# The low part of the last 64 activation rows, as 64-row products for two output blocks at once

## The chip, the cores and the metric

The kernel runs on one core of a Trainium2 chip. The metric is the device time of one execution in microseconds (us), and the median of several runs is quoted. Engines are named as in the profile: PE is TensorE (PEld its weight loads), DVE is VectorE, ACT is ScalarE, POOL is GpSimd and SP is SyncE, which issues most DMA transfers.

## The reference, cut to what matters

A recurrent attention gives 3072 rows of 320 features. Two expert layers follow; the change is in the second.

```python
def _moe_ref(x, w1, w2, w3, w_out):                 # d_ff 768
    h = np.maximum(np.maximum(x @ w1, x @ w2), x @ w3)
    return (h @ w_out).astype(np.float32)

def _moe2_ref(x, w_a, w_b, w_out):                  # d_ff 1536
    a = x @ w_a
    b = x @ w_b
    return (a * b @ w_out).astype(np.float32)
```

## The kernel before, in words

**Two parts of every number.** The weights arrive in 64-bit floats and the activations in 32-bit. Products are made in the 32-bit type fp32r, which TensorE takes at one column a step but rounds. So each operand is split into a high part and a low part, and a product is the sum of high x high, low x high and high x low.

**The second expert** (`moe_b(n)`, line 1039) runs for six groups n of 512 rows of x. The 320 features are the contraction: 128 + 128 + 64. The first two blocks have tiles `bxhi` and `bxlo` for the activations' parts and `bw` for the weights'. The last 64 features stand twice, in partitions 0 to 63 and again in 64 to 127: `bxt` holds their high part and `bxl` their low part. The matching weight tile `bt` holds the high part of the weights in partitions 0 to 63 and the low part in 64 to 127, so that one product over 128 partitions adds high and low weights at once.

For each of 12 blocks ff of 128 hidden units the work is:

- `l3` twice (line 1061), once for w_a and once for w_b: eight products of 512 columns that sum into one PSUM bank, six with `bw`, then `bt` with `bxt`, then `bt` with `bxl`;
- ACT copies the first bank (line 1087), DVE multiplies it with the second (line 1088), ACT makes the high part `bgh` (line 1090) and DVE the low part `bgl` by a subtraction (line 1091);
- `l4` (line 1072): twelve products of 320 columns into four output banks that stay open over all 12 blocks.

PSUM has eight banks: four for the outputs, four for the first products.

**Weights.** Of the 12 blocks, nine are split during the attention, written to DRAM and loaded again by `weights_b` (line 1018). The last three are split on the spot by `live_b` (line 1028) through `pieces` (line 846): four conversions of the raw 64-bit words on DVE (lines 841 to 844), copies of the high parts on ACT (lines 861 and 863), subtractions and additions for the low parts (lines 878 and 879). With two raw tiles a block this is sixteen DVE instructions.

**The order.** All work is entered as operations with costs, keys that are read and written, and priorities; `Plan.run` then lays them out greedily and emits each engine's instructions in that order. An operation that needs PSUM banks (`ps`) is placed only when it can have all of them, and banks of kind "b" are limited to four. When the planner expects PE to stand idle before its 650th microsecond, it emits fill: 128x128 products of the identity with itself into a free bank (line 320). They are ordinary instructions that PE has to run. A tile change is charged through the mark `md`.

Of the kernel before, what the change touches and what calls it, by code (L numbers as in the profile page):

```python
# [8 lines left out]
F32 = mybir.dt.float32  # L9
# [17 lines left out]
LV = 9  # L27
# [41 lines left out]
class Plan:  # L69
# [30 lines left out]
    def run(self, limit):  # L100
# [27 lines left out]
        done, last, top = 0, 0, 0.0  # L128
        line, port, mode = 0.0, 0.0, None
        itime, ileft = 0.0, ICAP  # L130
        count = lambda o: 0 if not o["md"] else 64 if o["md"] == "c64" and o["act"] > 0.42 else 128
        busy = {}

        state = [False]
# [147 lines left out]
def body(nc, tc, ia, out_ap):  # L282
# [17 lines left out]
    def dma(fn, nbytes, r=(), w=(), pri=0.0, pre=1.2):  # L300
        return op("SP", XISS, fn, r=r, w=w, pri=pri, lat=XWAY, pre=pre, xfer=nbytes / XRATE)
# [544 lines left out]
    def pieces(src, m, raw, ca, kr, ka, parts, WK, pri, summed=False, behind=None, need=()):  # L846

        rv = lambda: raw().bitcast(U32)[:, 0:2 * m].rearrange("p (m k) -> p m k", k=2)
        f = lambda k, c, n, r0, q: rv()[r0:r0 + q, c:c + n, k].bitcast(F32)
        if behind is None:  # L850
            dma(lambda w_: SP.dma_start(rv(), src.bitcast(U32).rearrange("p (m k) -> p m k", k=2)), 128 * m * 8, r=list(need), w=[kr], pri=pri)
        else:
            adma(lambda w_: A.dma_start(rv(), src.bitcast(U32).rearrange("p (m k) -> p m k", k=2)), 128 * m * 8, w=[kr], pri=pri, after=[behind])
        convert(rv, ca, m, kr, ka, pri)
        for i, (h, l, c, n, r0, q) in enumerate(parts):
            W = WK[i] if isinstance(WK, list) else WK
            k = (kr, "h", i)
            g_ = (lambda v: v.rearrange("p (k c) -> p k c", k=2)) if n > 512 else (lambda v: v)
            f = lambda k, c, n, r0, q, g_=g_: g_(rv()[r0:r0 + q, c:c + n, k].bitcast(F32))
            a = lambda c=c, n=n, r0=r0, q=q, g_=g_: g_(ca()[r0:r0 + q, c:c + n])  # L860
            last = op("ACT", ac(n), lambda w_, f=f, h=h, c=c, n=n, r0=r0, q=q: A.activation(h(), f(1, c, n, r0, q), AF.Copy), r=[kr], w=[k, W], pri=pri)
            if r0:
                op("ACT", ac(n), lambda w_, f=f, l=l, c=c, n=n, r0=r0, q=q: A.activation(l(), f(1, c, n, r0, q), AF.Copy), r=[kr], w=[k, W], pri=pri)
                h = l
            if summed:

                pn = ("a", "cv", next(serial))
                ro = 64 if q == 64 else 0
                o_ = lambda w_, pn=pn, n=n, ro=ro, q=q: bank[w_[pn]][ro:ro + q, 0:n]
                op("PE", n * 0.0035, lambda w_, f=f, h=h, c=c, n=n, r0=r0, q=q, o_=o_: (  # L870
                    T.matmul(o_(w_), ident[r0:r0 + q, r0:r0 + q], f(1, c, n, r0, q), start=True, stop=False),
                    T.matmul(o_(w_), nid[r0:r0 + q, r0:r0 + q], h().bitcast(F32), start=False, stop=False)),
                   r=[kr, k, "nid", "con"], w=[pn], ps=[pn], pri=pri, act=0.9)
                op("PE", n * 0.00175, lambda w_, f=f, c=c, n=n, r0=r0, q=q, o_=o_: T.matmul(o_(w_), ident[r0:r0 + q, r0:r0 + q], f(0, c, n, r0, q), start=False, stop=True),
                   r=[kr, "con"], w=[pn], pri=pri, act=0.9)
                op("ACT", ac(n), lambda w_, l=l, o_=o_: A.activation(l(), o_(w_), AF.Copy), r=[pn], w=[W, k], fin=[pn], pri=pri)
                continue
            sub = lambda E, f=f, h=h, a=a, c=c, n=n, r0=r0, q=q: (lambda w_: E.tensor_tensor(a(), f(1, c, n, r0, q), h(), ALU.subtract))
            add = lambda E, f=f, l=l, a=a, c=c, n=n, r0=r0, q=q: (lambda w_: E.tensor_tensor(l(), a(), f(0, c, n, r0, q), ALU.add))
            op("POOL", po(n), sub(G), r=[kr, k], w=[ka], pri=pri, alt=[("DVE", dv(n), sub(V))])  # L880
            op("POOL", po(n), add(G), r=[kr, ka], w=[W], pri=pri, alt=[("DVE", dv(n), add(V))])
        return last
# [81 lines left out]
    def bweights(w, k, nw):  # L964
        tb["bw", k] = w.tile([128, nw, 2, 512], F32R, name=f"bw{k}")
        tb["bt", k] = w.tile([128, nw, 256], F32R, name=f"bt{k}")
        tb["bo", k] = w.tile([128, nw, 2, DM], F32R, name=f"bo{k}")

    def wb(t, ff):
# [48 lines left out]
    def weights_b():  # L1018
        need = ["WB"]
        for ff in range(LV):  # L1020
            d = [("WD", ff, 0, i) for i in range(2)]
            dma(lambda w_, ff=ff: SP.dma_start(wb("bw", ff).bitcast(F32), WD[ff, :, :, 0:512].rearrange("k p c -> p k c")), 524e3, r=d + need, w=[("bW", ff)], pri=0.7)
            for i in range(2):
                dma(lambda w_, ff=ff, i=i: SP.dma_start(wb("bt", ff).bitcast(F32)[64 * i:64 * i + 64].rearrange("p (w c) -> p w c", w=2),
                                                        WD[ff, i, :, 512:640].rearrange("(w p) c -> p w c", w=2)), 66e3, r=d + need, w=[("bT", ff, i)], pri=0.7)
            dma(lambda w_, ff=ff: SP.dma_start(wb("bo", ff).bitcast(F32), WD[ff, :, :, 640:960].rearrange("k p c -> p k c")), 328e3, r=d + need, w=[("bO", ff)], pri=0.7)

    def live_b():

        for ff in range(LV, 12):  # L1030
            for q, (c0, m) in enumerate(((0, 512), (512, 448))):
                if q == 0:
                    parts = [(lambda ff=ff: wb("bw", ff)[:, 0], lambda ff=ff: wb("bw", ff)[:, 1], 0, 512, 0, 128)]
                else:
                    parts = [(lambda ff=ff, w=w: wb("bt", ff)[0:64, 128 * w:128 * w + 128], lambda ff=ff, w=w: wb("bt", ff)[64:128, 128 * w:128 * w + 128], 0, 128, 64 * w, 64) for w in range(2)]
                    parts.append((lambda ff=ff: wb("bo", ff)[:, 0], lambda ff=ff: wb("bo", ff)[:, 1], 128, DM, 0, 128))
                pieces(ia["wpb"][ff][:, c0:c0 + m], m, lambda q=q: tb["lr", q], lambda q=q: tb["lc", q], ("lr", q), ("lc", q), parts, ("bL", ff, q), 0.5, need=["WB"] if ff < NW else ["XB"])

    def moe_b(n):
# [21 lines left out]
        def l3(w_, ff, wi, pn):  # L1061
            ps = bank[w_[pn]]
            bh, bl = (wb("bw", ff)[:, k].rearrange("p (k c) -> p k c", k=2) for k in range(2))
            t2 = wb("bt", ff)
            cs = slice(wi * 128, wi * 128 + 128)
            h, l = tb["xhi", i], tb["xlo", i]
            seq = [(bh[:, 0, cs], h[:, 0]), (bh[:, 1, cs], h[:, 1]), (bl[:, 0, cs], h[:, 0]), (bl[:, 1, cs], h[:, 1]),
                   (bh[:, 0, cs], l[:, 0]), (bh[:, 1, cs], l[:, 1]), (t2[:, cs], tb["xt2", i]), (t2[:, cs], tb["xl2", i])]
            for k, (w, x) in enumerate(seq):
                T.matmul(ps, w, x, start=(k == 0), stop=(k == 7))  # L1070

        def l4(w_, ff):
            gh, gl = tb["gh", ff % 3], tb["gl", ff % 3]
# [8 lines left out]
        for ff in range(12):  # L1082
            j, k = ff % 2, ff % 3
            pa, pb = ("b", "ba", n, ff), ("b", "bb", n, ff)
            op("PE", 8 * 0.231, lambda w_, ff=ff, pa=pa: l3(w_, ff, 0, pa), r=xk + ([("bW", ff), ("bT", ff, 0), ("bT", ff, 1)] if ff < LV else [("bL", ff, 0), ("bL", ff, 1)]), w=[pa, ("gh", k)], ps=[pa], pri=pr)
            op("PE", 8 * 0.231, lambda w_, ff=ff, pb=pb: l3(w_, ff, 1, pb), r=xk + ([("bW", ff), ("bT", ff, 0), ("bT", ff, 1)] if ff < LV else [("bL", ff, 0), ("bL", ff, 1)]), w=[pb, ("gl", k)], ps=[pb], pri=pr)
            op("ACT", ac(512), lambda w_, j=j, pa=pa: A.activation(tb["as", j], bank[w_[pa]], AF.Copy), r=[pa], w=[("bas", j)], fin=[pa], pri=ep)  # L1087
            op("DVE", dv(512, True), lambda w_, j=j, pb=pb: V.tensor_tensor(tb["as", j], bank[w_[pb]], tb["as", j], ALU.mult),  # L1088
               r=[pb], w=[("bas", j)], fin=[pb], pri=ep)
            op("ACT", ac(512), lambda w_, j=j, k=k: A.activation(tb["gh", k], tb["as", j], AF.Copy), r=[("bas", j)], w=[("gh", k)], pri=ep)  # L1090
            op("DVE", dv(512), lambda w_, j=j, k=k: V.tensor_tensor(tb["gl", k], tb["as", j], tb["gh", k], ALU.subtract),  # L1091
               r=[("bas", j), ("gh", k)], w=[("gl", k)], pri=ep)
            op("PE", 1.757, lambda w_, ff=ff: l4(w_, ff), r=[("gh", k), ("gl", k), ("bO", ff) if ff < LV else ("bL", ff, 1)],
               w=po_, ps=po_ if ff == 0 else (), pri=pr)
# [251 lines left out]
```

## Time and profile before

| | us |
|---|---|
| median of 3 runs | 1049.93 (1048.65 to 1052.36) |
| the profiled execution | 1043.9 |
| its span on the core | 1042.0 |
| PE busy | 1011.2 (97%) |
| DVE busy | 623.5 (60%) |
| ACT busy | 501.7 (48%) |

The profiled execution is one of its own and lies somewhat below the median of the three runs. The attention and the first expert fill the span up to about 641 us, the second expert the rest. Records of products overlap, since the next product enters the array while the last one drains; what a product costs is therefore the distance from one start to the next, not the length of its record. A plain fp32 product leaves two records, an fp32r product one.

### The profile page before, as it was taken

The numbers are of one execution on the slowest core, as the hardware profiler recorded it, in microseconds if no ns is written. First come the engines' busy times: TensorE is split into PE (matmuls) and PEld (weight loads), VectorE is DVE, ScalarE is ACT, GpSimd is POOL, SyncE is SP. The second block draws the span as 40 slices with busy tenths as digits, with TensorE's granted clock in tenths as the row PEclk, the third lists the DMA queues.
The fourth block names the chain that finished last, engine by engine and source line by source line (L and its number), as shares of the span: only waits on it lengthen the run. The fifth ranks groups of instructions, "written<-read, shape, count | busy, mean of one in ns | idle before, by whom it ended". The sixth has DMA issues, their size and how long they took to land.

```text
span 1042.0 us, 34646 instructions
## 1 busy us (share of the span) xinstructions
PE 1011.2 (97%) x15200; PEld 913.6 (88%) x15200; DVE 623.5 (60%) x1014; ACT 501.7 (48%) x1143; POOL 140.8 (14%) x115
## 2 busy tenths in 40 slices
PE   8999999999988989999899999999999999999997
PEld 8877888989978989898899999888888888888886
DVE  7987888989786778887685523763232232322222
ACT  4267786668683848847476222342232222322221
POOL 3101113343151321331110000000000000000000
PEclk9999999999999999999999999999999999999999
DMA  8756767665766576675456387322020000000000
GB/s 236 165 133 165 180 147 167 126 150 154 164 147 156 118 200 126 169 166 148 122 143 176 129 231 211 103 56 61 1 56 1 1 26 1 26 1 1 26 1 28
DMA packets 165180, 115.01 MB, mean 110 GB/s; under 512 B 121632, under 2 KB 140704, under 8 KB 164064
## 3 DMA queue, kind: packets, MB, share of 16 engines
q1 hardware_dynamic: 163728, 108.31, 42.0%
q10 hardware_dynamic: 1296, 4.42, 1.1%
q8 instruction: 121, 1.98, 0.9%
q14 instruction: 35, 0.29, 0.1%
HBM read 85.10 MB, written 27.59 MB: 108 GB/s over the span
## 4 chain that ended last, share of the span: by engine, by line
PE 90%; DMA 3%; ACT 2%; DVE 2%; issue 2%; POOL 1%; SPq 1%; POOLq 0%; DVEq 0%
PE bank L1070 26%; PE bank L916 18%; PE bank L320 6%; PE bank L1080 4%; PE bank L1078 4%; PE bank L1079 4%; PE bank L811 3%; PE bank L793 2%; PE bank L491 2%; DMA KT<-in_kb_dram 2%; PE bank L941 2%; PE bank L652 2%; PE bank L635 2%; PE bank L942 2%; PE bank L678 2%
## 5 line engine op out<-in xcount | busy, mean ns | idle before, releaser
L1088 DVE TENSOR_TENSOR bas<-bank,bas 128x512 f32<-128x512 f32 x72 | 49.8, 692 | 197.4 <-PE bank L1070 191.0
L1070 PE MATMUL bank<-bxhi,bw 128*128 128x512 f32 x576 | 156.4, 393 | 0.0
L1070 PEld LDWEIGHTS bank<-bxhi,bw 128*128 128x128 f32 x576 | 106.1, 188 | 20.7
L1090 ACT ACTIVATE bgh<-bas 128x512 fp32r<-128x512 f32 x72 | 45.6, 633 | 144.2 <-DVE bas L1088 144.2
L1087 ACT ACTIVATE bas<-bank 128x512 f32<-128x512 f32 x72 | 43.1, 599 | 118.6 <-PE bank L1070 118.5
L916 PE MATMUL bank<-xhi,whi 128*128 128x256 f32 x432 | 94.6, 301 | 0.0
L1070 PE MATMUL bank<-bxlo,bw 128*128 128x512 f32 x288 | 89.7, 393 | 0.0
L1078 PE MATMUL bank<-bo,bgh 128*128 128x320 f32 x288 | 88.9, 309 | 0.0
L1080 PE MATMUL bank<-bo,bgl 128*128 128x320 f32 x288 | 88.9, 309 | 0.0
L1079 PE MATMUL bank<-bo,bgh 128*128 128x320 f32 x288 | 88.8, 308 | 0.0
L916 PE MATMUL bank<-xlo,whi 128*128 128x256 f32 x432 | 87.1, 283 | 0.0
L916 PE MATMUL bank<-xhi,wlo 128*128 128x256 f32 x432 | 87.1, 283 | 0.0
L931 DVE TENSOR_TENSOR hm<-bank,hm 128x512 f32<-128x512 f32 x72 | 49.6, 688 | 54.0 <-PE bank L916 50.0
L1091 DVE TENSOR_TENSOR bgl<-bas,bgh 128x512 fp32r<-128x512 f32 x72 | 50.9, 707 | 45.2 <-ACT bgh L1090 45.1
L320 PE MATMUL bank<-con 128*128 128x128 f32 x538 | 70.8, 285 | 5.9 <-DMA con<-in_con_dram 2.9
L320 PEld LDWEIGHTS bank<-con 128*128 128x128 f32 x538 | 65.3, 197 | 9.9 <-ACT bank L389 2.9
L916 PEld LDWEIGHTS bank<-xhi,whi 128*128 128x128 f32 x432 | 66.6, 191 | 2.8
L916 PEld LDWEIGHTS bank<-xhi,wlo 128*128 128x128 f32 x432 | 67.3, 192 | 0.0
L916 PEld LDWEIGHTS bank<-xlo,whi 128*128 128x128 f32 x432 | 67.3, 192 | 0.0
L1070 PEld LDWEIGHTS bank<-bxlo,bw 128*128 128x128 f32 x288 | 54.0, 188 | 12.4
L916 PE MATMUL bank<-xt,wt 128*128 128x256 f32 x216 | 61.2, 283 | 0.0
L916 PE MATMUL bank<-xl,wt 128*128 128x256 f32 x216 | 61.0, 282 | 0.0
(183 smaller groups left out, 2285.8 us busy)
## 6 DMA issues: line engine op xcount, KB each, us to landing
wraw<-in_wpb_dram SPq DMA_DIRECT2D x9, 960.0 KB
KT<-in_kb_dram SPq DMA_DIRECT2D x20, 384.0 KB
wraw<-in_wpa_dram SPq DMA_DIRECT2D x6, 768.0 KB
bw<-WD SPq DMA_DIRECT2D x9, 512.0 KB
WD<-wraw ACTq DMA_DIRECT2D x9, 480.0 KB
WD<-wca SPq DMA_DIRECT2D x9, 480.0 KB
Wp<-in_wf_dram SPq DMA_DIRECT2D x20, 198.4 KB
ZR<-in_vz_dram SPq DMA_DIRECT2D x48, 80.0 KB
```

Of the source, the lines that this page charges most:

```text
L320: P.keep = lambda b: T.matmul(bank[b][:, 0:128], ident, ident, start=True, stop=True)
L811: T.matmul(ps[64 * g:64 * g + 40, c0:c0 + 32], Y_[:, x, u, g], YL[:, x, u, g], start=True, stop=True)
L916: T.matmul(ps, w, x, start=(i == 0), stop=(i == 7))
L931: op("DVE", dv(512, True), lambda w_, pn=pn: V.tensor_tensor(f(hm), bank[w_[pn]], f(hm), ALU.max), r=[pn], w=["hm"], fin=[pn], pri=ep)
L1070: T.matmul(ps, w, x, start=(k == 0), stop=(k == 7))
L1078: T.matmul(o, gh[:, c], oh, start=ff == 0, stop=False)
L1079: T.matmul(o, gh[:, c], ol, start=False, stop=False)
L1080: T.matmul(o, gl[:, c], oh, start=False, stop=ff == 11)
L1087: op("ACT", ac(512), lambda w_, j=j, pa=pa: A.activation(tb["as", j], bank[w_[pa]], AF.Copy), r=[pa], w=[("bas", j)], fin=[pa], pri=ep)
L1088: op("DVE", dv(512, True), lambda w_, j=j, pb=pb: V.tensor_tensor(tb["as", j], bank[w_[pb]], tb["as", j], ALU.mult), r=[pb], w=[("bas", j) ...
L1090: op("ACT", ac(512), lambda w_, j=j, k=k: A.activation(tb["gh", k], tb["as", j], AF.Copy), r=[("bas", j)], w=[("gh", k)], pri=ep)
L1091: op("DVE", dv(512), lambda w_, j=j, k=k: V.tensor_tensor(tb["gl", k], tb["as", j], tb["gh", k], ALU.subtract), r=[("bas", j), ("gh", k)], ...
```

## The change

The product of `bt` with `bxl` goes. A new tile `bh` holds, for each block ff, only the high part of the weights of the last 64 features: w_a in partitions 0 to 63 and w_b in 64 to 127. For two blocks ff and ff + 1 together, a new operation `rest` issues four products over 64 partitions each, alternating between the upper and lower half, into the four banks of the two blocks. It opens the banks, and `l3` with its seven remaining products adds to them. The product of the low weights with the low activations is no longer made. `rest` asks for all four banks at once, and for `bh` of both blocks. `bh` is loaded by one more DMA for each of the nine stored blocks; for the other three, ACT makes it with one more copy, while one copy into `bt` goes.

```diff
-        count = lambda o: 0 if not o["md"] else 64 if ...
+        count = lambda o: 0 if not o["md"] or o["md"] == "r64" else 64 if ...
...
-        for i, (h, l, c, n, r0, q) in enumerate(parts):
+        for i, (h, l, c, n, r0, q, *more) in enumerate(parts):
...
-            if r0:
+            for x in more:
+                op("ACT", ac(n), lambda w_, f=f, x=x, c=c, n=n, r0=r0, q=q: A.activation(x(), f(1, c, n, r0, q), AF.Copy), r=[kr], w=[k, W], pri=pri)
+                h = x
+            if r0 and not more:
...
+        tb["bh", k] = w.tile([128, nw, 128], F32R, name=f"bh{k}")
...
+            dma(lambda w_, ff=ff: SP.dma_start(wb("bh", ff).bitcast(F32), WD[ff, 0, :, 512:640]), 66e3, r=d + need, w=[("bT", ff, 2)], pri=0.7)
...
-            seq = [(bh[:, 0, cs], h[:, 0]), (bh[:, 1, cs], h[:, 1]), (bl[:, 0, cs], h[:, 0]), (bl[:, 1, cs], h[:, 1]),
-                   (bh[:, 0, cs], l[:, 0]), (bh[:, 1, cs], l[:, 1]), (t2[:, cs], tb["xt2", i]), (t2[:, cs], tb["xl2", i])]
+            seq = [(t2[:, cs], tb["xt2", i]), (bh[:, 0, cs], h[:, 0]), (bh[:, 1, cs], h[:, 1]), (bl[:, 0, cs], h[:, 0]), (bl[:, 1, cs], h[:, 1]),
+                   (bh[:, 0, cs], l[:, 0]), (bh[:, 1, cs], l[:, 1])]
             for k, (w, x) in enumerate(seq):
-                T.matmul(ps, w, x, start=(k == 0), stop=(k == 7))
+                T.matmul(ps, w, x, start=False, stop=(k == 6), skip_group_check=True)
+
+        def rest(w_, ff, pn):
+            for k in range(4):
+                r = slice(64 * (k % 2), 64 * (k % 2) + 64)
+                T.matmul(bank[w_[pn[k]]], wb("bh", ff + k // 2)[r], tb["xl2", i][r], start=True, stop=False, skip_group_check=True)
...
+            if not j:
+                pn = [("b", x, n, f) for f in (ff, ff + 1) for x in ("ba", "bb")]
+                op("PE", 0.6, lambda w_, ff=ff, pn=pn: rest(w_, ff, pn), md="r64", r=[("bxl2", i), hk(ff), hk(ff + 1)], w=pn, ps=pn, pri=pr)
+            for wi, pn in enumerate((pa, pb)):
+                op("PE", 7 * 0.231, lambda w_, ff=ff, wi=wi, pn=pn: l3(w_, ff, wi, pn), r=xk + wk(ff), w=[pn, (("gh", "gl")[wi], k)], pri=pr)
```

The planner lays the second expert out anew. Up to its first product PE's instructions are as before. The following pieces show three places of the new order. On PE, in the first group, this is the end of block 1, and the first products of blocks 2 and 3, in the kernel before (lines 1070 and 1078 are `l3` and `l4`):

```order
L1070 MATMUL bank_64<-bxhi_10180,bw_10176 128x512 x4
L1070 MATMUL bank_64<-bxlo_10181,bw_10176 128x512 x2
L1070 MATMUL bank_64<-bxt_10182,bt_10177 128x512
L1070 MATMUL bank_64<-bxl_10183,bt_10177 128x512
L1070 MATMUL bank_63<-bxhi_10180,bw_10176 128x512 x4
```

After the change, on PE, ahead of blocks 2 and 3 (line 1090 is the last product of an `l4`, 1080 is `rest`, 1075 is `l3`):

```order
L1089 MATMUL bank_69<-bo_10179,bgh_10189 128x320
L1090 MATMUL bank_69<-bo_10179,bgl_10190 128x320
L1080 MATMUL bank_65<-bxl_10184,bh_10178 128x512
L1080 MATMUL bank_66<-bxl_10184,bh_10178 128x512
L1080 MATMUL bank_70<-bxl_10184,bh_10178 128x512
L1080 MATMUL bank_64<-bxl_10184,bh_10178 128x512
L1075 MATMUL bank_65<-bxt_10183,bt_10177 128x512
L1075 MATMUL bank_65<-bxhi_10181,bw_10176 128x512 x4
```

The 512-column product with `bxl` at the end of each bank has gone, and four 64-row products with `bxl` and `bh` stand ahead of two blocks, behind an `l4`.

Further on in the first group, still on PE after the change, `l3` of block 3 ends and `l4` of block 2 begins:

```order
L1075 MATMUL bank_64<-bxt_10183,bt_10177 128x512
L1075 MATMUL bank_64<-bxhi_10181,bw_10176 128x512 x4
L1075 MATMUL bank_64<-bxlo_10182,bw_10176 128x512 x2
L320 MATMUL bank_65<-con 128x128 x24
L1088 MATMUL bank_63<-bo_10179,bgh_10193 128x320
```

And where `l4` of block 3 ends and the `rest` of blocks 6 and 7 begins:

```order
L1089 MATMUL bank_69<-bo_10179,bgh_10189 128x320
L1090 MATMUL bank_69<-bo_10179,bgl_10190 128x320
L320 MATMUL bank_65<-con 128x128 x15
L1080 MATMUL bank_65<-bxl_10184,bh_10178 128x512
L1080 MATMUL bank_70<-bxl_10184,bh_10178 128x512
```

Between them are 24 and 15 fill products; before, the second expert had none.

On DVE, before, around the multiply of block 2 (line 1088) and the subtraction that makes its `bgl` (line 1091); lines 841 to 843 open the sixteen conversions of block 9:

```order
L1091 TENSOR_TENSOR bgl_10191<-bas_10187,bgh_10190 128x512
L1088 TENSOR_TENSOR bas_10186<-bank_68,bas_10186 128x512
L1091 TENSOR_TENSOR bgl_10193<-bas_10186,bgh_10192 128x512
L841 TENSOR_SCALAR blc_10197<-blr_10196 128x448
L842 SCALAR_TENSOR_TENSOR blr_10196<-blr_10196,blc_10197 128x448
```

After the change, on DVE, first the multiply of block 2 (now line 1103) and the start of the conversions:

```order
L1106 TENSOR_TENSOR bgl_10192<-bas_10188,bgh_10191 128x512
L1103 TENSOR_TENSOR bas_10187<-bank_66,bas_10187 128x512
L841 TENSOR_SCALAR blc_10198<-blr_10197 128x448
L842 SCALAR_TENSOR_TENSOR blr_10197<-blr_10197,blc_10198 128x448
L843 TENSOR_SCALAR blc_10198<-blr_10197 128x448
```

and, sixteen instructions behind that multiply, the end of the conversions and the subtraction of block 2 (now line 1106, `bgl_10194`):

```order
L881 TENSOR_TENSOR blc_10198<-blr_10197,bo_10720 128x320
L882 TENSOR_TENSOR bo_10720<-blc_10198,blr_10197 128x320
L882 TENSOR_TENSOR bw_10717<-blc_10196,blr_10195 128x512
L1106 TENSOR_TENSOR bgl_10194<-bas_10187,bgh_10193 128x512
L1103 TENSOR_TENSOR bas_10188<-bank_64,bas_10188 128x512
```

All sixteen conversions now stand between a block's multiply and its subtraction, which stood ahead of them.

## Rows read from the trace of the kernel before

**Rows 1.** Page, part 1: busy us (share of the span) and instructions

```profile
PE 1011.2 (97%) x15200; PEld 913.6 (88%) x15200; DVE 623.5 (60%) x1014; ACT 501.7 (48%) x1143; POOL 140.8 (14%) x115
```

**Rows 2.** Windows: stretch, length, busy by engine (instructions), clock, DMA share, GB/s

```profile
600.00:640.00 40.00, 40.00 (x336) 39.83 (x335) 14.19 (x23) 9.58 (x17) 0.00 (x0) 1.00 0.90 256
...
920.00:960.00 40.00, 40.00 (x206) 35.01 (x205) 9.69 (x14) 9.22 (x15) 0.00 (x0) 1.00 0.00 1
```

**Rows 3.** Chain of waits from 641 us to the end, share by line

```profile
by line: PE bank L1070 66.3%; PE bank L1080 10.5%; PE bank L1078 10.5%; PE bank L1079 10.5%; PE bank L943 0.1%; PE bank L942 0.1%; PE bank L941 0.1%; ACT bos L1098 0.1%; PE bank L944 0.1%; PE bank L945 0.1%; issue 0.0%
```

**Rows 4.** Groups by shape, PE: count, busy us and mean ns, idle before

```profile
L1070 PE MATMUL bank<-bxl,bt 128*128 128x512 f32 x144 | 56.5, 392 | 0.0
```

**Rows 5.** Timeline, steady second expert: start us, length us, engine, line, instruction, count

```profile
742.85 0.39 PE L1070 MATMUL bank<-bxl,bt 128*128 128x512 f32 x1
...
743.08 0.31 PE L1078 MATMUL bank<-bo,bgh 128*128 128x320 f32 x1
...
743.35 0.69 DVE L1088 TENSOR_TENSOR bas<-bank,bas 128x512 f32<-128x512 f32 x1 [5.16 <-PE bank L1070]
...
744.08 0.63 ACT L1090 ACTIVATE bgh<-bas 128x512 fp32r<-128x512 f32 x1 [2.00 <-DVE bas L1088]
...
744.74 0.69 DVE L1091 TENSOR_TENSOR bgl<-bas,bgh 128x512 fp32r<-128x512 f32 x1 [0.70 <-ACT bgh L1090]
744.84 1.10 PE L1070 MATMUL bank<-bxhi,bw 128*128 128x512 f32 x4
```

**Rows 6.** Timeline, PE, first expert with products on small tiles

```profile
346.07 0.28 PE L916 MATMUL bank<-xt,wt 128*128 128x256 f32 x1
346.19 0.28 PE L916 MATMUL bank<-xl,wt 128*128 128x256 f32 x1
346.40 0.79 PE L692 MATMUL bank<-Zs,TT 32*32 32x40 f32 x64
347.12 1.21 PE L793 MATMUL bank<-RB,XT 80*64 80x64 f32 x32
...
350.11 0.50 PE L916 MATMUL bank<-xhi,whi 128*128 128x256 f32 x2
350.45 0.40 PE L916 MATMUL bank<-xhi,wlo 128*128 128x256 f32 x2
```

**Rows 7.** Timeline, PE, around five fill products

```profile
616.85 0.28 PE L945 MATMUL bank<-hlo,woh 128*128 128x256 f32 x1
616.98 1.28 PE L320 MATMUL bank<-con 128*128 128x128 f32 x10
618.01 0.48 PE L916 MATMUL bank<-xhi,whi 128*128 128x256 f32 x2
```

**Rows 8.** Timeline, PE, early: 64-row tiles and fifty fill products

```profile
28.48 2.06 PE L491 MATMUL bank<-ZL,KT 40*64 40x32 f32 x64
30.47 1.16 PE L320 MATMUL bank<-con 128*128 128x128 f32 x8
...
33.54 11.43 PE L320 MATMUL bank<-con 128*128 128x128 f32 x100
44.81 0.84 PE L871 MATMUL bank<-wraw,con 128*128 128x384 f32 x2
```

**Rows 9.** Timeline, DVE: conversions of block 9, start of block 10's

```profile
656.26 0.39 DVE L841 TENSOR_SCALAR blc<-blr 128x448 uint32<-128x448 uint32 x1
...
662.67 0.49 DVE L879 TENSOR_TENSOR bo<-blc,blr 128x320 fp32r<-128x320 f32 x1
...
664.41 0.68 DVE L1088 TENSOR_TENSOR bas<-bank,bas 128x512 f32<-128x512 f32 x1
...
668.77 0.39 DVE L841 TENSOR_SCALAR blc<-blr 128x448 uint32<-128x448 uint32 x1
```

**Rows 10.** Timeline, SP: issues of raw weights for block 10

```profile
663.23 1.68 SPq L851 DMA_DIRECT2D blr<-in_wpb_dram  x2
```

**Rows 11.** Timeline, ACT: a copy of 64x128 among the conversions

```profile
657.34 0.32 ACT L861 ACTIVATE bt<-blr 64x128 fp32r<-64x128 f32 x1 [1.72 <-DVE blr L842]
```

More of the change, by code (lines that the diff above doesn't have):

```diff
@@ L130, in run @@
         itime, ileft = 0.0, ICAP
-        count = lambda o: 0 if not o["md"] else 64 if o["md"] == "c64" and o["act"] > 0.42 else 128
+        count = lambda o: 0 if not o["md"] or o["md"] == "r64" else 64 if o["md"] == "c64" and o["act"] > 0.42 else 128
         busy = {}
@@ L1034, in live_b @@
                 else:
-                    parts = [(lambda ff=ff, w=w: wb("bt", ff)[0:64, 128 * w:128 * w + 128], lambda ff=ff, w=w: wb("bt", ff)[64:128, 128 * w:128 * w + 128], 0, 128, 64 * w, 64) for w in range(2)]
+                    parts = [(lambda ff=ff, w=w: wb("bt", ff)[0:64, 128 * w:128 * w + 128], lambda ff=ff, w=w: wb("bt", ff)[64:128, 128 * w:128 * w + 128], 0, 128, 64 * w, 64, lambda ff=ff, w=w: wb("bh", ff)[64 * w:64 * w + 64]) for w in range(2)]
                     parts.append((lambda ff=ff: wb("bo", ff)[:, 0], lambda ff=ff: wb("bo", ff)[:, 1], 128, DM, 0, 128))
@@ L1084, in moe_b @@
             pa, pb = ("b", "ba", n, ff), ("b", "bb", n, ff)
-            op("PE", 8 * 0.231, lambda w_, ff=ff, pa=pa: l3(w_, ff, 0, pa), r=xk + ([("bW", ff), ("bT", ff, 0), ("bT", ff, 1)] if ff < LV else [("bL", ff, 0), ("bL", ff, 1)]), w=[pa, ("gh", k)], ps=[pa], pri=pr)
-            op("PE", 8 * 0.231, lambda w_, ff=ff, pb=pb: l3(w_, ff, 1, pb), r=xk + ([("bW", ff), ("bT", ff, 0), ("bT", ff, 1)] if ff < LV else [("bL", ff, 0), ("bL", ff, 1)]), w=[pb, ("gl", k)], ps=[pb], pri=pr)
+            wk = lambda ff: [("bW", ff), ("bT", ff, 0), ("bT", ff, 1), ("bT", ff, 2)] if ff < LV else [("bL", ff, 0), ("bL", ff, 1)]
+            hk = lambda ff: ("bT", ff, 2) if ff < LV else ("bL", ff, 1)
+            if not j:
[3 more added lines that the diff above has]
+                op("PE", 7 * 0.231, lambda w_, ff=ff, wi=wi, pn=pn: l3(w_, ff, wi, pn), r=xk + wk(ff), w=[pn, (("gh", "gl")[wi], k)], pri=pr)
             op("ACT", ac(512), lambda w_, j=j, pa=pa: A.activation(tb["as", j], bank[w_[pa]], AF.Copy), r=[pa], w=[("bas", j)], fin=[pa], pri=ep)
```

## The prediction

> **What bounds the kernel now.** I read the page's busy shares first: TensorE (PE) works 97% of the span, DVE 60% and ACT 48% [rows 1]. Next the busy time by stretch: from 600 us on PE is busy 40.00 of 40.00 us at a granted clock of 1.00, its upper level of 2.4 GHz; in the steady second expert DVE and ACT need only 9.69 and 9.22 of 40 us, while DMA is busy 0.90 of 600 to 640 us and idle later [rows 2]. The chain of waits from 641 us to the end is PE's alone: 66.3% on the first products of the second expert (line 1070) and 10.5% on each line of its second products; it names no wait of PE before the last output copy [rows 3]. So in the stage that is changed, time is what PE has to do, in the order in which it is queued. A microsecond taken from PE there is gained; one that is added is lost; a wait counts only where PE is not given something to do meanwhile.
>
> **The products that go.** 144 products read bxl against all 128 rows of bt [rows 4]. Their records are 0.39 us long, but they overlap: from the start of one to the start of the next is 0.23 us (742.85 to 743.08) [rows 5]. I use 0.231: the step is a little shorter in some stretches. Removed: 144 x 0.231 = 33.3 us.
>
> **The products that come.** Each of 36 new stretches has four 64-row products of 512 columns, alternating between the two halves of the rows and each into its own bank. If two run at once, four cost the stream of two: 0.46 us. Nothing in the trace runs 64-row, 128-column fp32r products, so the overlap is bounded from other tiles. Alone, a record of 128 columns of fill takes 11.27 us / 100 = 0.113 us, 0.88 ns a column (33.54 to 44.81) [rows 8]. Products on 32x32 tiles at line 692 have records of 40 columns, alone 35 ns; 64 of them take 0.72 us, 11 ns each (346.40 to 347.12) [rows 6], so about three run at once. Against it stands line 491, two tiles of 64 rows and 64 columns: 64 records of 32 columns, alone 28 ns, take 1.99 us, 31 ns each (28.48 to 30.47) [rows 8], no gain at all. I read those 31 ns as the price of loading 64 weight columns, one load after another, about 0.5 ns a column. Then four loads of 128 columns are 0.25 us, which the 0.46 us of streaming hide, but for the load that lets the second product of the first pair start late: 0.06 us. I take overlap, because line 692 shows row tiles side by side; without it a stretch streams 0.92 us.
>
> **The changes of tile.** Going into tiles, a product of 256 columns is followed after 0.21 us where its like follows after 0.12 (346.07, 346.19, 346.40): 0.09 more. Coming back, the first two products last 0.50 us, the next two 0.40: 0.10 more (350.11, 350.45) [rows 6]. But 0.08 of the way back also appears behind full-size fill, whose operands are plain fp32: the two products behind it last 0.48 us [rows 7]. So the two changes cost between some 0.03 and 0.19 us where everything is fp32r; I take 0.19, since both rows are real changes of tile. A stretch is then 0.46 + 0.06 + 0.19 = 0.71 us in place of 4 x 0.231 = 0.92, a gain of 0.21, and 36 of them 7.7 us.
>
> The Trainium skill (TensorEngine Tiling, Key Properties) says that a change of tiling mode drains the TensorE. The trace agrees only in part: the product that starts at 346.19 has a record of 0.28 us, so until 346.47, and the tile's first starts at 346.40 [rows 6]. By the rule the price would be the overhang of a 512-column record, 0.39 - 0.23 = 0.16 us at either end, and the sum 4.7 us higher; that is a rival below. The Trainium skill (TensorE: Matmul & The Clock Gate, Part 3) has products on different row groups start some 4 ns apart, which would take 36 x 0.056 = 2.0 us off the sum; no row here has such a pair.
>
> **What the planner adds.** The PE order now has two runs of fill (128x128 products with the identity, line 320) inside the second expert, 24 and 15, where there were none. They are unconditional work. Five such took 1.03 us, two records each (616.98 to 618.01) [rows 7], and fifty 11.27 us [rows 8]: 0.206 to 0.225 us each. 39 x 0.225 = 8.8 us (8.0 by the five). What put them there is the DVE order: DVE now does all sixteen conversions of the block of weights that is converted on the spot ahead of the subtraction that makes bgl of output block 2; before, that subtraction came first. These conversions last 8.15 us (656.26 to 664.41) [rows 9].
>
> Do the runs hide the wait, or does more come behind them? From the end of the last first-layer product of block 2, DVE needs 0.96 us until its multiply is done (743.08 to 743.35 + 0.69), 8.15 for the conversions, 0.69 for the subtraction and 0.1 to hand over: 9.9 us [rows 5, 9]. PE has 1.76 us of second products (743.08 to 744.84) [rows 5], 14 x 0.231 = 3.23 and 24 x 0.225 = 5.41: 10.4 us. No wait is left. At the second run the new stretch needs four banks at once, the last of which DVE frees behind the next sixteen conversions. From the second products of block 2, PE has 1.76 + 0.71 + 28 x 0.231 + 1.76 + 15 x 0.225 = 14.1 us; DVE and ACT have 2.1 (multiply, copy, subtraction: 0.69 + 0.63 + 0.69 and their hand-overs [rows 5]) + 8.15 + 1.4 for two multiplies = 11.7, and 2.4 us in which the raw weights may still be landing. They are issued 0.56 us after the start of their buffer's last reader and were in use 5.5 us after the issue (662.67, 663.23, 668.77) [rows 9, 10], against some 6.7 us here. So I take nothing beyond the fill, with up to 3 us if the transfers are late. Elsewhere the four banks cost nothing: the last is free 0.96 us after PE has gone on, and 1.76 us of second products stand ahead of each stretch.
>
> **Edits that cost nothing.** Nine loads of bh pass through SP's queue: an issue is 1.68 / 2 = 0.84 us by the two of [rows 10], 7.6 us in all, and 0.59 MB at the 256 GB/s of that stretch are 2.3 us [rows 2]. PE's first-expert backlog covers them until 641 us; without that cover they would cost up to 9.9 us. Three more ACT copies of 64x128, 0.32 us each [rows 11], lie within the conversions, where ACT waits for DVE anyway.
>
> **The sum.** -33.3 + 36 x 0.71 + 8.8 = +1.1 us. The profiled execution took 1043.9 us, 1042.0 of span and 1.9 around it, and would become 1045.0; that execution lies 6.0 below the median of the runs, 1049.93, and the difference is added there: 1051.0 us.
>
> **The rivals.**
> 1. Cheap stretches. The tile changes cost only 0.03 us, since the 0.08 belongs to fp32 operands and the entry likewise. A stretch is 0.46 + 0.06 + 0.03 = 0.55 us: -33.3 + 19.8 + 8.8 = -4.7 us, 1045.2. For it: the same 0.08 without a tile change. Against: the way in costs 0.09 though the work ahead of it is fp32r, and full-size fill behind such work starts after 0.13 us, without delay (616.85, 616.98) [rows 7].
> 2. A full drain at each change: 0.16 us twice, a stretch of 0.84 us, -33.3 + 30.2 + 8.8 = +5.7 us, 1055.6, slower. It decides as soon as the two changes cost more than some 0.25 us. For it: the overhang of 512-column records is longer than what was measured behind 256 columns. Against: the tile's start before the record's end.
> 3. The change doesn't do what it says: the halves run one after the other. 0.92 + 0.19 a stretch: -33.3 + 40.0 + 8.8 = +15.5 us, 1065.4. For it line 491, against it line 692.
> 4. Late raw weights or later DVE: +2 to +4 us on the forecast, 1053 to 1055.
>
> **How the numbers follow.** About 0.3%, 3.1 us, is what a measurement of this kernel can tell from no change. Forecast 0.50, rival 1 0.17, rival 2 0.15, rival 3 0.10, rival 4 0.08. The forecast's own spread (1047 to 1053) lies within 0.3%; half of rival 4 does too. So faster 0.17, same 0.53, slower 0.30. The range runs from rival 1, 1045, to above rival 2, 1058; it leaves out rival 3 and a little below.
>
> **What would show it.** In the profile after: pairs of 64-row records that start together or some 0.06 us apart, and not 0.23; a stretch of four from the product before to the product behind worth some 0.71 us; 39 fill products near 655 and 675 us and no wait of PE beside them; the same clock and no wait of PE later. The forecast is wrong if the pairs don't overlap, if the changes cost well under 0.1 or over 0.3 us a stretch, or if PE waits behind the fill.

## The result and the profile after

The kernel after took 1057.55 us (median of 9 runs, 1051.53 to 1062.78), the kernel before 1051.01 us beside it (median of 9 runs, 1047.19 to 1053.32). The ratio is 1.0059, 95% interval 1.0033 to 1.0085: slower by some 6.2 us, where 1.1 us had been forecast. The profiled execution took 1052.76 us, 1051.0 of it span.

For the stage that is changed there is a measure without the spread of the rest: from the start of its first product to the start of its last. It is called the stage below. These are the two products in the timeline of PE, before (start us, length us, engine, line, instruction, count; as in all timelines below):

```profile
641.12 1.08 PE L1070 MATMUL bank<-bxhi,bw 128*128 128x512 f32 x4
...
1035.28 0.31 PE L1080 MATMUL bank<-bo,bgl 128*128 128x320 f32 x1
```

and after:

```profile
643.58 0.50 PE L1080 MATMUL bank<-bxl,bh 64*128 64x512 f32 x2
...
1044.40 0.31 PE L1090 MATMUL bank<-bo,bgl 128*128 128x320 f32 x1
```

394.16 us before, 400.82 after: 6.66 us more, which is the whole difference of the medians and a little over. The stage begins 2.5 us later after, though PE's instructions ahead of it are the same; in the other profiled runs it begins anywhere from 641 to 653 us, so that is spread between executions. The stage itself hardly spreads: from the ninth stretch of 64-row products to the last product PE has the same 1580 products after and in experiments 1 and 2 below, and takes 305.27, 305.25 and 305.26 us for them in the three profiled executions. A median less its stage is 656.8 us before and 656.7 after.

The page's busy shares after, which answer to [rows 1]:

```profile
PE 1020.7 (97%) x15278; PEld 909.3 (87%) x15278; DVE 623.7 (59%) x1013; ACT 502.4 (48%) x1146; POOL 140.8 (13%) x116
```

The windows after, where [rows 2] stood before (stretch, length, busy by engine, clock, DMA share, GB/s):

```profile
640.00:680.00 40.00, 40.00 (x244) 34.96 (x242) 22.11 (x44) 12.05 (x25) 0.00 (x0) 1.00 0.50 137
680.00:720.00 40.00, 40.00 (x225) 34.20 (x224) 22.54 (x40) 14.72 (x28) 1.40 (x2) 1.00 0.20 56
920.00:960.00 40.00, 40.00 (x208) 33.41 (x208) 10.37 (x15) 9.31 (x16) 0.00 (x0) 1.00 0.00 1
```

PE is still busy all the time, at the same clock, and no wait of PE is found anywhere in the stage. So the time came from more work on PE, not from a wait. The chain of waits from 645 us to the end, share by line, is PE's as in [rows 3], now with 5.7% on the new products and 2.1% on fill:

```profile
by line: PE bank L1075 58.7%; PE bank L1088 10.6%; PE bank L1090 10.4%; PE bank L1089 10.4%; PE bank L1080 5.7%; PE bank L320 2.1%; PE bank L946 0.1%; PE bank L945 0.1%; PE bank L944 0.1%; ACT bos L1113 0.1%; PE bank L947 0.1%; PE bank L948
```

The groups by shape, PE, from 640 us on (count, busy us and mean ns, idle before), show what replaces [rows 4]:

```profile
L1080 PE MATMUL bank<-bxl,bh 64*128 64x512 f32 x144 | 26.4, 444 | 0.0
L320 PE MATMUL bank<-con 128*128 128x128 f32 x78 | 9.0, 275 | 0.0
```

The 144 products have 26.4 us of busy time against 56.5 before, since two of them now run at once; a reader who stopped here would expect a gain. Busy time counts overlapping records once and doesn't hold what a change of tile delays (a change between products over 128 rows and products over 64). One stretch in the timeline of all engines, the steps of which stand for all 36:

```profile
695.15 0.19 PEld L1090 LDWEIGHTS bank<-bo,bgl 128*128 128x128 f32 x1
...
695.29 0.31 PE L1090 MATMUL bank<-bo,bgl 128*128 128x320 f32 x1
...
695.53 0.30 PEld L1080 LDWEIGHTS bank<-bxl,bh 64*128 64x128 f32 x4 [0.19 <-issue]
695.53 0.73 PE L1080 MATMUL bank<-bxl,bh 64*128 64x512 f32 x4
...
696.19 0.19 PEld L1075 LDWEIGHTS bank<-bxt,bt 128*128 128x128 f32 x1 [0.36 <-issue]
696.19 0.50 PE L1075 MATMUL bank<-bxt,bt 128*128 128x512 f32 x1
696.30 0.65 PEld L1075 LDWEIGHTS bank<-bxhi,bw 128*128 128x128 f32 x3
696.53 0.63 PE L1075 MATMUL bank<-bxhi,bw 128*128 128x512 f32 x2
```

The steps from start to start, as medians over the 36 stretches in the trace's records: from the `l4` product ahead to the first pair 0.238 us, where its like follows after 0.147 (0.09 more); 4 ns between the two of a pair; from the first pair to the second 0.336 and not 0.231 (0.105 more); from the second pair to the full product behind 0.327 (0.096 more); from that product to its next 0.337 (0.106 more). Each change of tile thus costs twice: a late start of the first product behind it, and a late start of the second. A stretch is 0.46 + 0.40 = 0.86 us, against 0.92 for the four products that it replaced.

The PEld rows show where the second delay sits. In the ordinary stream a weight load starts at the start of the product before, here 0.14 us ahead of its own product (695.15 and 695.29). Behind a change the first product's load starts only with that product (695.53, 696.19), and the record of the product is 0.49 to 0.50 us long and not 0.39. The next load starts 0.11 us later (696.30) and its product 0.23 us behind that load (696.53), no later than a load of this stream ordinarily leads. So the time that the second product is late is, as far as the records tell, the first one's weight load, which nothing hides; that the load is the cause was not tested by an edit of its own.

The two runs of fill, in the timeline of PE after (two records to a product):

```profile
663.00 0.62 PE L1075 MATMUL bank<-bxlo,bw 128*128 128x512 f32 x2
663.46 5.52 PE L320 MATMUL bank<-con 128*128 128x128 f32 x48
668.73 0.39 PE L1088 MATMUL bank<-bo,bgh 128*128 128x320 f32 x1
...
679.56 3.51 PE L320 MATMUL bank<-con 128*128 128x128 f32 x30
682.99 0.73 PE L1080 MATMUL bank<-bxl,bh 64*128 64x512 f32 x4
```

5.27 and 3.43 us, 8.7 in all. And DVE beside them, which answers to [rows 9]:

```profile
658.77 0.69 DVE L1103 TENSOR_TENSOR bas<-bank,bas 128x512 f32<-128x512 f32 x1 [3.74 <-PE bank L1075]
659.38 0.38 DVE L841 TENSOR_SCALAR blc<-blr 128x448 uint32<-128x448 uint32 x1
...
667.07 0.68 DVE L1106 TENSOR_TENSOR bgl<-bas,bgh 128x512 fp32r<-128x512 f32 x1
...
670.74 0.39 DVE L841 TENSOR_SCALAR blc<-blr 128x448 uint32<-128x448 uint32 x1 [1.00 <-DMA blr<-in_wpb_dram]
...
680.60 1.28 DVE L1103 TENSOR_TENSOR bas<-bank,bas 128x512 f32<-128x512 f32 x2
```

The conversions last from 659.38 to 667.07, the subtraction behind them ends at 667.75, and the fill ends 1.0 us after that. The next raw weights are 1.00 us late for DVE (670.74), but the four banks are free at 681.88, before the second run of fill is over at 682.99. So both runs cover all that is late.

### The profile page after: what moved, and what is told of

The parts are those of the page before. It is cut to its first block, busy times and chain, and to the rows that moved or that the text cites. A ratio compares the mean times of both kernels' runs of the same rounds, so it can differ in the third digit from the quotient of the medians.

```text
span 1051.0 us, 34812 instructions
## 1 busy us (share of the span) xinstructions
PE 1020.7 (97%) x15278; PEld 909.3 (87%) x15278; DVE 623.7 (59%) x1013; ACT 502.4 (48%) x1146; POOL 140.8 (13%) x116
## 4 chain that ended last, share of the span: by engine, by line
PE 89%; DMA 3%; issue 2%; ACT 2%; DVE 2%; POOL 1%; SPq 1%; DVEq 0%; POOLq 0%
PE bank L1075 23%; PE bank L919 17%; PE bank L320 6%; PE bank L1088 4%; PE bank L1090 4%; PE bank L1089 4%; PE bank L811 3%; PE bank L1080 2%; PE bank L793 2%; PE bank L944 2%; DMA KT<-in_kb_dram 2%; PE bank L491 2%; PE bank L635 2%; PE bank L692 2%; PE bank L652 2%
## 5 line engine op out<-in xcount | busy, mean ns | idle before, releaser
L320 PE MATMUL bank<-con 128*128 128x128 f32 x616 | 80.2, 285 | 5.9 <-DMA con<-in_con_dram 3.0
L320 PEld LDWEIGHTS bank<-con 128*128 128x128 f32 x616 | 74.8, 197 | 9.8 <-ACT bank L389 2.9
L458 POOL TENSOR_TENSOR ZL<-ZL,Pp 64x512 f32<-64x512 f32 x29 | 41.1, 1418 | 149.2 <-DVE Pp L440 84.7
```

Source lines behind the costliest of these rows:

```text
L320: P.keep = lambda b: T.matmul(bank[b][:, 0:128], ident, ident, start=True, stop=True)
L458: op("POOL", po(512), lambda w_, cc=cc, g=g, r0=r0: G.tensor_tensor(Z_[r0:r0 + 64, cc, g], Z_[r0:r0 + 64, cc, g], P_[r0:r0 + 64, cc, :, 0: ...
```

## The experiments

The account to be tested has three terms: -33.3 us for the products that went, 36 x 0.86 = +30.9 for the stretches, +8.7 for the fill, together +6.3, against 6.66 of the stage. All diffs are against the kernel after. Timed kernels are compared by ratio with the kernel before, beside which they ran; the others by the stage of one profiled execution. The differences of some 2 us below are read from the stage too: the ratios, known to some 3 us, don't tell such kernels apart.

**1. The fill is left out** (label e1_no_fill), on every engine the same order otherwise.

```diff
-                            self.keep(banks[0][1])
+                            if a < 600.0: self.keep(banks[0][1])
...
-                        self.keep(banks[0][1])
+                        if s < 600.0: self.keep(banks[0][1])
```

> The changed kernel with the same order on every engine, but the 39 fill products of the second expert are not issued. Measured by the second expert alone, from the start of its first product to the start of its last (before 394.2 us, after 400.8). Theory, the fill stands where PE would wait anyway: PE then waits about 4.2 us for bgl of block 2, until DVE's subtraction ends some 4.3 us after the last first-layer product, and about 2.4 us for the fourth bank of blocks 6 and 7; the stage falls by 1 us or so, to 399 to 400, unless the granted clock drops in the wait, which would make it longer. Rival, the fill is a cost of its own: the stage falls by all of its 8.7 us, to 392.

Measured: 1059.77 us (7 runs), ratio 1.0096 [1.0058, 1.0135]; the stage 402.60 us, longer than with the fill. PE's waits in the stage (us, times, longest):

```profile
PE bank L1090 <- DVE bgl L1106: 3.9, 1, 3.9
PE bank L1080 <- DVE bas L1103: 1.2, 1, 1.2
```

Its windows:

```profile
640.00:680.00 40.00, 36.09 (x209) 31.20 (x208) 20.00 (x37) 9.96 (x19) 0.00 (x0) 0.92 0.64 181
680.00:720.00 40.00, 38.71 (x186) 31.91 (x185) 21.55 (x40) 14.06 (x29) 1.40 (x2) 0.95 0.16 45
```

And PE's timeline at the first wait:

```profile
670.05 0.30 PE L1089 MATMUL bank<-bo,bgh 128*128 128x320 f32 x1
674.27 0.64 PE L1090 MATMUL bank<-bo,bgl 128*128 128x320 f32 x1 [3.91 <-DVE bgl L1106]
674.70 0.47 PE L1088 MATMUL bank<-bo,bgh 128*128 128x320 f32 x1
674.97 0.47 PE L1089 MATMUL bank<-bo,bgh 128*128 128x320 f32 x1
```

The expectation of 399 to 400 us missed on the other side, and the exception that it named, a falling clock, is what came. Of the 8.7 us of fill 5.1 come back as the two waits, and the clock does the rest: the granted clock is 0.92 and 0.95 of these two stretches of 40 us, and behind the wait products of 320 columns follow one another after 0.27 us (674.70 to 674.97) and not 0.147, the lower level of 1.2 GHz (320 columns in 0.267 us). If the missing 0.08 and 0.05 are time at half clock, that is 6.4 + 4.0 us, in which 5.2 us of work are lost; the profile has a granted clock of 0.50 from 673.6 to 680.4 us and from 690.7 to 694.0, and 1.00 between. -8.7 + 5.1 + 5.2 = +1.6, against the 1.8 measured. So the fill is not the cost; the late subtraction is, and with this order of DVE the fill is cheaper than the bare wait.

**2. The conversions are put later** (label e2_late_conversions): the three blocks that are converted on the spot get a later priority each, so that the planner takes the subtractions between the conversions.

```diff
-  pieces(ia["wpb"][ff]..., ("bL", ff, q), 0.5, need=...)
+  pieces(ia["wpb"][ff]..., ("bL", ff, q), (1.0, 0.9, 0.8)[ff - LV], need=...)
```

> The changed kernel with lower priorities for the on-the-spot conversions (1.0, 0.9 and 0.8 for blocks 9, 10 and 11, not 0.5), so that DVE makes bgl of block 2 after two conversions and not after sixteen; the planner then puts no fill into the second expert. Theory, the 8.7 us of fill and the waits that it stands for come from the order of DVE alone: the stage is 392 to 393.5 us, no wait of PE beyond 1.2 us, 36 stretches as before at some 0.86 us each, and the time 1 to 2.5 us below the kernel before (ratio 0.9976 to 0.999). Rival, the 64-row products are what makes the kernel slower, and DVE is late elsewhere: the stage stays above 394.2.

Measured: 1047.54 us (12 runs, 1042.31 to 1056.0), ratio 0.9969 [0.9942, 0.9997]; the stage 392.83 us. There is no fill in the stage, and one wait:

```profile
PE bank L1090 <- DVE bgl L1106: 0.4, 1, 0.4
```

DVE in its timeline, where all sixteen conversions had stood ahead of the subtraction:

```profile
659.48 0.69 DVE L1103 TENSOR_TENSOR bas<-bank,bas 128x512 f32<-128x512 f32 x1 [3.73 <-PE bank L1075]
660.09 0.38 DVE L841 TENSOR_SCALAR blc<-blr 128x448 uint32<-128x448 uint32 x1
661.05 0.68 DVE L1106 TENSOR_TENSOR bgl<-bas,bgh 128x512 fp32r<-128x512 f32 x1
```

As expected: 400.82 - 392.83 = 8.0 us of the stage are the order of DVE. This version is faster than the kernel after and, by an interval that ends just below 1, than the kernel before; of the 3.3 us by which the ratio puts it ahead the stage accounts for 394.16 - 392.83 = 1.3, the rest is within the interval.

**3. Full rows in the stretches** (label e3_full_rows): order and fill as after, but the four products read all 128 rows (and so wait for `bt` in place of `bh`); no tile changes.

```diff
-  T.matmul(bank[w_[pn[k]]], wb("bh", ff + k // 2)[r], tb["xl2", i][r], ...)
+  T.matmul(bank[w_[pn[k]]], wb("bt", ff + k // 2)[:, 128 * (k % 2):128 * (k % 2) + 128], tb["xl2", i], ...)
```

> The changed kernel, but the four products of a stretch take all 128 rows of bt and bxl, as before the change; order and fill stay. No tile changes. Theory, a stretch of 64-row pairs costs 0.86 us and four full products 0.92: the stage grows by 36 x 0.07 = 2.4 us to 403.2. Rival, the tile changes cost what the prediction gave them (0.25 with the late second product, a stretch of 0.71): it grows by 7.7 to 408.5. Rival, they cost more than pairing saves: it falls below 400.8.

Measured: 1058.61 us (10 runs), ratio 1.0072 [1.0038, 1.0106]; the stage 402.98 us. PE's timeline around a stretch:

```profile
700.50 0.31 PE L1090 MATMUL bank<-bo,bgl 128*128 128x320 f32 x1
700.65 1.09 PE L1080 MATMUL bank<-bxl,bt 128*128 128x512 f32 x4
701.57 0.40 PE L1075 MATMUL bank<-bxt,bt 128*128 128x512 f32 x1
```

The stretch starts 0.15 us after the product ahead, the ordinary step, where the 64-row one of after waited 0.24. Full rows cost 402.98 - 400.82 = 2.2 us more; 36 x (0.924 - 0.858) = 2.4 had been reckoned. So in the place where they stand the 64-row products are a gain, and a small one.

**4. All four products of a stretch on the upper half** (label e4_same_half). The last 64 rows' low part is then taken with w_a's weights for w_b too, so that part of w_b's sums is another quantity.

```diff
-                r = slice(64 * (k % 2), 64 * (k % 2) + 64)
+                r = slice(0, 64)
```

> The changed kernel, but all four products of a stretch read the upper 64 rows (so the outputs of w_b get the wrong last 64 features of the low activations). Theory, two products run at once because they lie on different halves of the rows: now they follow one another, 4 x 0.23 of streaming in place of 2 x 0.23, and the stage grows by 36 x 0.46 = 16.6 us to 417.4. Rival, a 64-row product simply takes half the time on any rows: the stage stays at 400.8.

Measured: the stage 417.15 us (1070.86 us in one run). PE's timeline:

```profile
710.43 0.31 PE L1090 MATMUL bank<-bo,bgl 128*128 128x320 f32 x1
710.67 1.19 PE L1080 MATMUL bank<-bxl,bh 64*128 64x512 f32 x4
711.79 0.50 PE L1075 MATMUL bank<-bxt,bt 128*128 128x512 f32 x1
```

The four follow one another after 0.336, 0.232 and 0.234 us (means): one after the other, at the step of full products, with the 0.105 at the first. 417.15 - 400.82 = 16.3 us is 36 x 0.454, two more streams of 0.23 a stretch. Two of these products run at once only on different halves, and what a change of tile costs is about the same with and without that (0.39 us a stretch here by the same steps, 0.40 after).

**5. The same four products in the order upper, upper, lower, lower** (label e5_same_half_first).

```diff
-            for k in range(4):
+            for k in (0, 2, 1, 3):
```

> The changed kernel, but the four products of a stretch go out in the order upper, upper, lower, lower half (both blocks' w_a, then both blocks' w_b); the sums are the same. Theory, products are taken in order and two run at once only where neighbours in the queue lie on different halves: only the middle two overlap, a stretch streams 3 x 0.23 us and not 2 x 0.23, and the second expert grows from 400.8 by 36 x 0.23 = 8.3 us to 409.1. Rival, TensorE pairs them whatever their order: it stays at 400.8.

Measured: the stage 401.06 us (1059.0 us in one run); the theory fell, and the rival held.

```profile
725.03 0.31 PE L1090 MATMUL bank<-bo,bgl 128*128 128x320 f32 x1
725.27 0.73 PE L1080 MATMUL bank<-bxl,bh 64*128 64x512 f32 x4
725.94 0.50 PE L1075 MATMUL bank<-bxt,bt 128*128 128x512 f32 x1
```

The instructions stand in the program as upper, upper, lower, lower (for blocks 2 and 3 of the first group banks 65, 70, 66, 64, where the kernel after has 65, 66, 70, 64). Yet the stretch has the same length, with the steps 7, 336 and 8.5 ns: two still run at once. Served strictly in order, the two upper ones would have had 0.336 us between them and the last two another 0.23, as in experiment 4. The records don't name the halves, but the trace keeps which semaphores each weight load waits for. By these the loads start in the order upper, lower, upper, lower: all 36 stretches fit it, and 31 of them don't fit the order of the program (in the other five the two orders wait for the same). So a lower load, and with it the product that starts right behind it, passed the upper one that stood ahead of it. What swaps them between the program and the array, the trace doesn't say.

**6. A stretch for each block** (label e6_stretch_per_block): two products, one pair, 72 stretches; a block then needs neither the other's `bh` nor four banks (the planner is also told 0.37 us for it in place of 0.6).

```diff
-            for k in range(4):
+            for k in range(2):
...
-            if not j:
-                pn = [("b", x, n, f) for f in (ff, ff + 1) for x in ("ba", "bb")]
+            if True:
+                pn = [("b", x, n, ff) for x in ("ba", "bb")]
```

> The changed kernel, but each output block has a stretch of its own with two products and two banks: 72 stretches of one pair, not 36 of two; DVE makes bgl of block 2 ahead of the conversions again and the planner puts no fill into the second expert. Theory, a stretch pays 0.40 us for its two tile changes however little it holds: the second expert is 394.2 - 33.3 + 72 x (0.23 + 0.40) = 406.2 us, though it has no fill. Rival, the changes cost the 0.25 us of the prediction: 395.5. Rival, what costs is asking for four banks at once: it falls under 394.2.

Measured: the stage 406.52 us (1056.19 us in one run), with no fill in it and no wait of PE. PE's timeline around one stretch:

```profile
710.36 0.31 PE L1090 MATMUL bank<-bo,bgl 128*128 128x320 f32 x1
710.60 0.50 PE L1080 MATMUL bank<-bxl,bh 64*128 64x512 f32 x2
711.03 0.51 PE L1075 MATMUL bank<-bxt,bt 128*128 128x512 f32 x1
711.37 0.86 PE L1075 MATMUL bank<-bxhi,bw 128*128 128x512 f32 x3
```

Here the stage is -33.3 + 72 x (0.23 + c) longer than before, so c = (406.52 - 394.16 + 33.3) / 72 - 0.23 = 0.40 us: the price of the two changes of tile, found a second time with twice as many of them and without fill. The old order of DVE is back, too (multiply at 655.00, subtraction at 656.39, first conversion at 657.00): it was the taking of two blocks together that moved the conversions.

**7. Late conversions and full rows** (label e7_late_full_rows), experiments 2 and 3 together.

> The kernel of e2 with the four products of a stretch over all 128 rows, on the same order of every engine: no 64-row products, no tile changes. Theory, the 64-row products themselves are worth 36 x (0.924 - 0.858) = 2.4 us once DVE's order is mended: the second expert is 392.8 + 2.4 = 395.2 us, the time that of the kernel before within 0.3%. Rival, e2 owes its gain to its order alone: it stays at 392.8.

Measured: 1053.63 us (10 runs), ratio 1.0031 [0.9998, 1.0065]; the stage 394.94 us, with the same wait of 0.4. Against experiment 2 the 64-row products alone are worth 394.94 - 392.83 = 2.1 us, near the 2.2 of experiment 3. The medians of the two lie 6.1 us apart; the 4 us that are not in the stage lie ahead of it, where the executions spread, and are not explained, beyond that the two ratios were measured on different chips and each is known to some 3 us.

## Why the prediction was right and where it was wrong

The time fell in the range, and on the side of slower, to which 0.30 had been given; the forecast itself was 5.1 us too low (+1.1 where +6.2 was measured), and the likeliest outcome by the prediction, no change, didn't come. The range reaches up to the measured time only because it takes in rival 2, whose price is made up otherwise than what was found; that it reached so far is in part luck.

- **What bounds the stage**: right. PE is busy 40.00 of 40.00 us, and the stage is the sum of what stands in its order (6.3 worked out, 6.66 measured).
- **The products that go**, 144 x 0.231: right. The step is 0.231 us in the median of all first products before, and experiment 3, which keeps the four in their new place, has a stage of 394.16 + 8.7 = 402.9 by it, and 402.98 measured.
- **Two at once**: right, and better than taken. The two of a pair start 4 ns apart, so the 0.06 us for a late second product, read from line 491 [rows 8], was wrong. The Trainium skill (TensorE: Matmul & The Clock Gate, Part 3) gives those 4 ns; the trace agrees.
- **The changes of tile**: this is the term that was mis-sized, 0.19 us a stretch where 0.40 was measured, 36 x 0.21 = 7.6 us; less the 36 x 0.056 = 2.0 us of the point above and 0.1 of fill, that is 5.5 of the 5.6 by which the stage exceeded the sum. [rows 6] showed the way in only as the delay of the first product in the tile, since those behind it are 40 columns wide and too many to tell a second delay; and of the way back I took the 0.10 by which one pair of records was longer, and no more. Each change costs 0.09 us at the first product and 0.105 at the second, as far as the records tell by the first one's weight load. The delay that I had at each end was thus half of what is paid. The way back could have been priced from the trace before, where the first full product behind the small tiles of [rows 6] is followed after 0.224 us by the second, and that one after the ordinary 0.12 (narrow windows of PE's timeline, in which the two records are not merged):

```profile
350.11 0.38 PE L916 MATMUL bank<-xhi,whi 128*128 128x256 f32 x1
350.34 0.28 PE L916 MATMUL bank<-xhi,whi 128*128 128x256 f32 x1
350.45 0.28 PE L916 MATMUL bank<-xhi,wlo 128*128 128x256 f32 x1
```

That is the 0.10 taken for the whole return; over the 34 returns to line 916 from the tiles of lines 692, 705 and 793 the median is 0.22. What was left out is that the first full product starts late as well, 0.13 us behind the last small one at these returns, where small ones follow one another after some 0.01.

- **Rival 2**, a full drain: near in its price (+5.7 us, 0.84 a stretch), not in what makes it up. A stretch starts before the record ahead of it ends (695.53, where that record runs from 695.29 to 695.60, though the ends of records are modelled), so the first product of a change is 0.09 to 0.10 us late and not the overhang of 0.16, and whether that much is a drain is not shown; the other half of the 0.40 comes at the second products, which the rival did not have. Its point of decision, two changes at more than some 0.25 us, was passed.
- The Trainium skill (TensorEngine Tiling (Array Packing), Key Properties) says that a change of tiling mode drains the engine. That there is a price at each change the traces bear out; the 0.105 us at the second product behind a change, over half of the price, is not in that sentence.
- **The fill**: right, 8.7 us for 8.8. **No wait left behind it**: right in either place, and the raw weights came 1.00 us late without effect. What the prediction didn't see is what the fill was worth: it treated 39 products as a pure addition, and experiment 1 shows that without them the kernel is slower still by 1.8 us of its stage.

## What to carry to other kernels

Halving the rows of a few products pays only if the stretch between two changes of tile is long: at 0.40 us for the pair of changes and 0.231 us for each product of 512 columns that overlap saves, a stretch of four wins 0.06 us and one of two loses 0.17. Price a change from the starts of the two products behind it, not from busy time and not from the first alone. And look at the whole order: the arithmetic won 2 us, and one more dependence between two blocks, through the order of another engine, cost 8.

## What of the hardware was not expected

- Behind each change between 128-row and 64-row products the second product comes 0.105 us late: the first one's weights are not loaded ahead (PEld at 695.53 and 696.19, where the ordinary load leads by 0.14 us), and its record is 0.10 us longer.
- Products on the two halves start 4 ns apart, and they still pair when two on the same half are queued ahead of the two on the other (steps of 7 and 8.5 ns, stage 401.06 against 400.82): the weight loads start in the order upper, lower, upper, lower and not in the program's.
- A wait of 3.9 us brought the granted clock down: products of 320 columns took 0.27 us a step behind it, and 0.147 elsewhere. That is some 5 us of work lost behind 5.1 us of waits.
